# GpSimd's normalisation of attention rows: one instruction with two tensors, or four instructions with one scalar per row

## The chip, the cores and the metric

One core of one Trainium2 chip runs the whole program. The metric is the device time of one execution in microseconds; lower is better. The core has five engines, called here by the profile's names: PE (TensorE, matrix products), DVE (VectorE), ACT (ScalarE), POOL (GpSimd) and SP (SyncE, which here only issues DMA transfers). Each engine works through its own list of instructions in order and waits at the head of the list for what the next instruction needs.

## The reference

Sliding-window attention over 8 batches, 8 heads, 576 positions and head size 64, and behind it a two-layer network with squared ReLU over all 4608 tokens. All of it is float32.

```python
scores = scale * np.matmul(q, k.transpose(0, 1, 3, 2))
bias = slopes[:, None, None] * (-np.abs(rel).astype(np.float32))[None, :, :]
mask = (rel >= 0) & (rel < window)            # window = 128
scores = np.where(mask, scores + bias[None], -1000000000.0)
scores = scores - np.max(scores, axis=-1, keepdims=True)
attn = np.exp(scores)
attn = attn / (np.sum(attn, axis=-1, keepdims=True) + 1e-09)
out = np.matmul(attn, v)
x = out.transpose(0, 2, 1, 3).reshape(4608, 512)
h = np.maximum(x @ w_in, 0.0)                 # w_in 512 x 2048
return h * h @ w_out                          # w_out 2048 x 512
```

The division by the row sums is the step that the change touches. The kernel does it as a multiplication by reciprocals.

## The kernel before, in words

The 4608 tokens are cut into 9 chunks of 512. For each chunk the network needs 16 first products (`gemm1`, one per 128 of the 2048 hidden columns, 12 matmuls each, L200) and 16 second products (`gemm2`, L229, 12 matmuls each); `gemm2` of a hidden block runs two blocks behind its `gemm1`. Between the two, ACT takes the ReLU (`r`, L210), DVE squares it (`r<-r`, L213), ACT rounds it to a high part (`hh`, L217) and DVE takes the rest (`hl`, L219).

Attention is done in segments: a pair of heads times 256 tokens, held as a tile `t` of 128 query rows by 4 blocks of columns. Two segments, s = 0 and s = 1, make a `Couple`, and four couples make the input of one chunk. There are two forms.

- The first eight segments (`Wide`, in the first 40 us) are set out by a planner (`Plan.run`, `start`): it gives PE, DVE, ACT, POOL and SP an order by due times and its own costs. Here a row block has 256 columns (or 128 where the first half is masked away); the normalised blocks are turned by PE (L620, L623).
- From couple 4 on a segment's blocks have 128 columns each. DVE adds distances and takes maxima (L250), ACT takes exponentials with row sums (L257), DVE turns the four sums of a row into reciprocals (`nm`, L264 and L265), POOL multiplies the four blocks of `t` by them (`norm`, L268), DVE transposes 32 x 32 blocks of the result into `pp` (L319, STREAM_TRANSPOSE), SP writes that to DRAM in four transfers (`way<-pp`, L323) and reads it back in one (`pp<-way`, L328), and POOL cuts the square into its two triangles (two affine selects, L332).

From couple 9 on, past 150 us, the couples' matmuls come in a **visit** (function `visit`): once every 8 products, that is every 23.65 us, PE interrupts the network's products to multiply the old couple's triangles with the values (L539) and to make the new couple's scores (L546). The visit's new couple goes through the steps above during the 23 us that follow, s = 0 first, s = 1 behind it, and its four triangles are due at the next visit. There are 28 visits; called visit 0 (at 156.21 us) to visit 27 (at 797.63 us) here. Visits 1 to 27 each use a couple that passed through `norm` in the period before.

What stands around the change in each engine's list past 150 us: PE's order is written out by hand. The order of DVE, ACT, POOL and SP there is made by a scheduler that runs over the program with its own estimates of durations; a changed instruction can therefore move its neighbours. On SP the order within one period is: four writes of s = 0, the read of s = 0, four writes of s = 1, the read of s = 1. The writes of s = 1 stand behind the read of s = 0, which waits for its own writes to land.

The two functions of the change are `Segment.norm` (L267, the couples) and `Wide.norm` (L605, the first eight segments); segment 7 of these (`NORMS`) is normalised on DVE, one block at a time with a scalar per row, before and after.

Of the kernel before, what the change touches and what calls it, by code (L numbers as in the profile page):

```python
# [14 lines left out]
ALU = mybir.AluOpType  # L15
# [26 lines left out]
NORMS = (7,)  # L42
# [196 lines left out]
class Segment:  # L239
# [25 lines left out]
        self.nc.vector.reciprocal(rec, rec)  # L265

    def norm(self):  # L267
        self.nc.gpsimd.tensor_tensor(  # L268
            self.t, self.t, self.nm[:, 8:12].unsqueeze(2).to_broadcast([128, 4, 128]), op=ALU.mult
        )  # L270

    def turn(self):
        self.place()
# [285 lines left out]
class Wide(Segment):  # L559
# [45 lines left out]
    def norm(self):  # L605
        for i in (0, 1) if self.skip else (None,):
            m, a = (slice(None), 0) if i is None else (slice(i, 4, 2), self.first[i])
            t, rec = self.t[:, m, a:256], self.nm[:, 8:12][:, m]
            if self.k in NORMS:
                for j in range(t.shape[1]):  # L610
                    self.nc.vector.tensor_scalar(t[:, j], t[:, j], rec[:, j : j + 1], None, op0=ALU.mult)
                continue
            self.nc.gpsimd.tensor_tensor(t, t, rec.unsqueeze(2).to_broadcast(list(t.shape)), op=ALU.mult)

    def turn(self):
        self.place()
# [271 lines left out]
```

## Time and profile before

| | |
|---|---|
| median of 3 runs | 895.94 us (895.66 to 896.19) |
| profiled execution | 895.99 us |
| its span | 894.3 us |
| mean granted clock of PE | 0.999 |
| PE busy | 883.3 us (99%) |
| DVE / ACT / POOL busy | 496.7 / 419.0 / 200.0 us |
| `norm` of the couples (L268) | 64 instructions, 69.0 us busy |
| `norm` of the first segments (L613) | 11 instructions on POOL |

The profiled execution took 1.69 us more than the span of its instructions, and 0.05 us more than the median. A row of a timeline gives the start in us from the beginning of the span, the length in us, the engine, the line of the program, the operation with output and input, and how many instructions the row merges; in square brackets stands how long the engine was idle before it and what ended that. A row of the grouped view gives, after the bar, the busy time in us, the mean length of one instruction in ns, and the idle time before them. "SPq" marks SP's issuing of a transfer, not the transfer itself.

### The profile page before, as it was taken

The page shows a single profiled execution, that of the slowest core. Times are in us where ns is not written, and L with a number is a line of the kernel's source. Part 1 is how long each engine was busy: PE and PEld are TensorE (multiplying, and loading weights), DVE is VectorE, ACT ScalarE, POOL GpSimd, SP SyncE. Part 2 cuts the span into 40 slices and gives each one's busy share as a digit, 9 for nine tenths or more (in the row PEclk, how much of TensorE's full clock was granted, in tenths as well). Part 3 has the DMA queues.
Part 4 walks back from the last instruction along what each step waited for, and adds up shares of the span by engine and source line. Part 5 has one row for each costly group of instructions (what it writes and reads, how often), then busy time and mean ns, then how long its engine had stood idle before and what let it go on. Part 6 is the DMA issues. An engine that isn't in the chain of part 4 may idle for free.

```text
span 894.3 us, 19481 instructions
## 1 busy us (share of the span) xinstructions
PE 883.3 (99%) x7488; PEld 780.6 (87%) x7492; DVE 496.7 (56%) x1326; ACT 419.0 (47%) x1115; POOL 200.0 (22%) x255
## 2 busy tenths in 40 slices
PE   8899999999999999999999999999999999999998
PEld 5678888999899999999899989998999999989997
DVE  5999884555655555555545565555555555533222
ACT  7899753444444444334444444444444454323222
POOL 3222332222222222222222222212222222220000
PEclk9999999999999999999999999999999999999999
DMA  9985333332332334233422243333422331211001
GB/s 345 403 332 177 92 113 110 89 90 80 107 107 77 89 89 129 86 90 89 130 69 76 89 136 89 89 90 85 129 75 81 89 102 45 49 48 48 0 1 48
DMA packets 72893, 95.26 MB, mean 107 GB/s; under 512 B 8032, under 2 KB 41952, under 8 KB 72800
## 3 DMA queue, kind: packets, MB, share of 16 engines
q1 hardware_dynamic: 72368, 93.36, 33.9%
q8 instruction: 59, 0.97, 0.5%
q10 hardware_dynamic: 432, 0.66, 0.2%
q14 instruction: 34, 0.28, 0.1%
HBM read 67.76 MB, written 26.21 MB: 105 GB/s over the span
## 4 chain that ended last, share of the span: by engine, by line
PE 95%; ACT 3%; DVE 2%; issue 1%; POOLq 0%; DVEq 0%; ACTq 0%
PE acc L229 42%; PE g L200 42%; PE s L539 5%; PE g L546 2%; ACT tw L596 1%; PE s L546 1%; PE at L344 1%; PE g L132 0%; PE s L410 0%; ACT t L468 0%; PE at L410 0%; DVE tw L589 0%; DVE raw L178 0%; DVE pp L627 0%; ACT raw L176 0%
## 5 line engine op out<-in xcount | busy, mean ns | idle before, releaser
L200 PE MATMUL g<-xu,w 128*128 128x512 f32 x1728 | 400.9, 381 | 1.8 <-DVE xu L528 0.9
L200 PEld LDWEIGHTS g<-xu,w 128*128 128x128 f32 x1728 | 339.4, 197 | 39.6 <-DVE xu L528 2.3
L229 PE MATMUL acc<-hh,w 128*128 128x512 f32 x1152 | 371.1, 384 | 0.0
L229 PEld LDWEIGHTS acc<-hh,w 128*128 128x128 f32 x1152 | 225.9, 196 | 28.7 <-issue 5.3
L210 ACT ACTIVATE r<-g 128x512 f32<-128x512 f32 x144 | 86.0, 597 | 305.6 <-PE g L200 299.1
L229 PE MATMUL acc<-hl,w 128*128 128x512 f32 x576 | 219.2, 381 | 0.0
L213 DVE TENSOR_TENSOR r<-r 128x512 f32<-128x512 f32 x129 | 89.0, 690 | 225.7 <-ACT r L210 225.4
L219 DVE TENSOR_TENSOR hl<-r,hh 128x512 fp32r<-128x512 f32 x144 | 122.9, 854 | 78.3 <-ACT hh L217 78.1
L332 POOL TENSOR_SCALAR_AFFINE_SELECT pp<-pp 128x512 f32<-128x512 f32 x128 | 105.3, 823 | 230.2 <-DMA pp<-way 192.6
L217 ACT CAST hh<-r 128x512 fp32r<-128x512 f32 x144 | 89.2, 619 | 82.3 <-DVE r L213 80.8
L268 POOL TENSOR_TENSOR t<-t,nm 128x512 f32<-128x512 f32 x64 | 69.0, 1078 | 255.2 <-DVE nm L265 243.2
L229 PEld LDWEIGHTS acc<-hl,w 128*128 128x128 f32 x576 | 113.3, 197 | 11.6
L257 ACT ACTIVATE t<-t,nm 128x128 f32<-128x128 f32 x256 | 99.9, 393 | 12.2 <-DVE nm L250 12.1
L319 DVE STREAM_TRANSPOSE pp<-t 128x512 f32<-128x512 f32 x64 | 45.0, 705 | 35.9 <-POOL t L268 35.8
L250 DVE CUSTOM_DVE_ANT_0 t<-t,cst 128x128 f32<-128x128 f32 x256 | 59.1, 295 | 1.0
L539 PE MATMUL s<-pp,v 64*64 64x128 f32 (+1 forms) x1792 | 52.2, 248 | 0.1
L539 PEld LDWEIGHTS s<-pp,v 64*64 64x64 f32 x1792 | 40.7, 134 | 9.5 <-issue 8.4
L257 ACT ACTIVATION_READ_ACCUMULATOR t<-t,nm 128x1 f32 x256 | 48.3, 189 | 0.0
L480 DVE COPY_PREDICATED t<-cst,s 64x256 f32<-64x256 int32 x100 | 44.4, 444 | 6.5 <-ACT t L461 3.6
L527 ACT CAST xu<-s 128x512 fp32r<-128x512 f32 x28 | 16.4, 586 | 41.5 <-DVE t L480 26.6
L468 ACT COPY t<-g 64x256 f32<-64x256 f32 (+2 forms) x86 | 28.0, 340 | 3.9 <-PE g L546 1.2
L470 POOL MEMSET t<- 64x128 f32 (+1 forms) x44 | 10.0, 229 | 87.7 <-PE s L546 79.3
(71 smaller groups left out, 482.0 us busy)
## 6 DMA issues: line engine op xcount, KB each, us to landing
raw<-in_dram SPq DMA_DIRECT2D x32, 512.0 KB, 8.7
way<-pp SPq DMA_DIRECT2D x256, 64.0 KB, 2.0
pp<-way SPq DMA_DIRECT2D x64, 256.0 KB, 2.7
qk<-in_dram SPq DMA_DIRECT2D x32, 320.0 KB, 3.1
v<-in_dram SPq DMA_DIRECT2D x32, 320.0 KB, 3.9
qk<-in_dram SPq DMA_DIRECT2D x38, 256.0 KB, 4.2
out_dram<-o SPq DMA_DIRECT2D x35, 256.0 KB, 2.7
v<-in_dram SPq DMA_DIRECT2D x3, 256.0 KB, 4.9
```

Source lines behind the costliest of these rows:

```text
L200: nc.tensor.matmul(g, w, in_turn(c, xs[cc][:, part]), start=i == 0, stop=i == 11)
L210: self.relu = nc.scalar.activation(r, g, AF.Relu)
L213: nc.vector.tensor_tensor(r, r, r, op=ALU.mult)
L217: nc.scalar.copy(hh, r)
L219: nc.vector.tensor_tensor(hl, r, hh.bitcast(F32), op=ALU.subtract)
L229: nc.tensor.matmul(self.acc[m], w, in_turn(c, h), start=(f == 0 and i == 0), stop=(f == NF - 1 and i == 2))
L250: self.nc.vector.tensor_tensor_reduce(self.t[:, m], self.t[:, m], self.K.nrel(2 * self.p + m // 2), -0.125, BIG, ALU.add, ALU.min, self.nm ...
L257: return self.nc.scalar.activation(self.t[:, m], self.t[:, m], AF.Exp, bias=nm[:, m : m + 1], scale=-1.0, accum_out=nm[:, 4 + m : 5 + m],)
L268: self.nc.gpsimd.tensor_tensor(self.t, self.t, self.nm[:, 8:12].unsqueeze(2).to_broadcast([128, 4, 128]), op=ALU.mult)
L319: nc.vector.transpose(squares.rearrange("p b m c -> p m b c"), self.t.rearrange("p m (b c) -> p m b c", c=32))
L332: nc.gpsimd.affine_select(to, self.own, pattern=[[-32 * sign, 4], [0, 4], [-sign, 32]], compare_op=op, fill=0.0, base=0, channel_multiplie ...
L539: made.append(mm(to, w, x, start=first and n < 2, stop=not first, skip_group_check=True))
```

## The change

`norm` multiplies each of the four blocks by its own column of reciprocals, in four instructions whose second operand is one scalar per row, where one instruction (two in `Wide` segments with masked halves) took the tile and the reciprocals, repeated along the columns, as two tensors. What is multiplied by what is the same.

```diff
     def norm(self):
-        self.nc.gpsimd.tensor_tensor(
-            self.t, self.t, self.nm[:, 8:12].unsqueeze(2).to_broadcast([128, 4, 128]), op=ALU.mult
-        )
+        for m in range(4):
+            self.nc.gpsimd.tensor_scalar(self.t[:, m], self.t[:, m], self.nm[:, 8 + m : 9 + m], None, op0=ALU.mult)
...
             t, rec = self.t[:, m, a:256], self.nm[:, 8:12][:, m]
-            if self.k in NORMS:
-                for j in range(t.shape[1]):
-                    self.nc.vector.tensor_scalar(t[:, j], t[:, j], rec[:, j : j + 1], None, op0=ALU.mult)
-                continue
-            self.nc.gpsimd.tensor_tensor(t, t, rec.unsqueeze(2).to_broadcast(list(t.shape)), op=ALU.mult)
+            engine = self.nc.vector if self.k in NORMS else self.nc.gpsimd
+            for j in range(t.shape[1]):
+                engine.tensor_scalar(t[:, j], t[:, j], rec[:, j : j + 1], None, op0=ALU.mult)
```

Three lines fewer stand ahead of L613, so line numbers past it are lower by three in the changed program (L268 is L269, L319 is L318).

On POOL the couples' stretch stood as follows (t is a segment's probabilities, nm its sums and reciprocals, pp the transposed square):

```order
L332 AFFINE_SELECT pp<-pp 128x512 x4
L268 TENSOR_TENSOR t<-t,nm 128x512 x2
L470 MEMSET t 64x2x64 x2
L332 AFFINE_SELECT pp<-pp 128x512 x4
L268 TENSOR_TENSOR t<-t,nm 128x512 x2
```

and now stands:

```order
L331 AFFINE_SELECT pp<-pp 128x512 x4
L269 TENSOR_SCALAR t<-t,nm 128x128 x8
L469 MEMSET t 64x2x64 x2
L331 AFFINE_SELECT pp<-pp 128x512 x4
L269 TENSOR_SCALAR t<-t,nm 128x128 x8
```

Each pair of instructions became eight; nothing else on POOL moved. PE's and ACT's lists are the same as before. On DVE the lists are the same up to 140 us; past that, some neighbours of the STREAM_TRANSPOSE moved. Before, every couple's period had this order on DVE, from the last step of the old couple (xu) on:

```order
L528 TENSOR_TENSOR xu<-s,xu 128x512
L264 TENSOR_SCALAR nm<-nm 128x4
L265 RECIPROCAL nm<-nm 128x4
L319 STREAM_TRANSPOSE pp<-t 128x4x4x32
L213 TENSOR_TENSOR r<-r 128x512
L264 TENSOR_SCALAR nm<-nm 128x4
L265 RECIPROCAL nm<-nm 128x4
L219 TENSOR_TENSOR hl<-r,hh 128x512
L319 STREAM_TRANSPOSE pp<-t 128x4x4x32
L213 TENSOR_TENSOR r<-r 128x512
L219 TENSOR_TENSOR hl<-r,hh 128x512
```

In 13 of the 27 periods (those ahead of visits 12 to 21 and 24 to 26, **order A** in what follows) it still has. Ahead of visits 1 to 7 and 27 (**order B**) the square `r` stands ahead of the first transpose, and the rest is as before. Ahead of visits 8 to 11, 22 and 23 (**order C**) more moved:

```order
L527 TENSOR_TENSOR xu<-s,xu 128x512
L264 TENSOR_SCALAR nm<-nm 128x4
L265 RECIPROCAL nm<-nm 128x4
L213 TENSOR_TENSOR r<-r 128x512
L318 STREAM_TRANSPOSE pp<-t 128x4x4x32
L264 TENSOR_SCALAR nm<-nm 128x4
L219 TENSOR_TENSOR hl<-r,hh 128x512
L265 RECIPROCAL nm<-nm 128x4
L213 TENSOR_TENSOR r<-r 128x512
L318 STREAM_TRANSPOSE pp<-t 128x4x4x32
L219 TENSOR_TENSOR hl<-r,hh 128x512
```

There the second reciprocal, which lets POOL begin on s = 1, stands behind `hl`, and the second transpose stands behind the next block's `r`. Ahead of visit 8 a copy of an output tile (`o<-acc`, L235 before) stands ahead of that `r` too. On SP, about 150 us into the run, two output writes moved ahead of a read of `pp`; and in the period ahead of visit 8 two output writes, which stood behind the four writes of s = 1, now stand ahead of them, and two more ahead of the read of s = 1. The rest of its list is unchanged.

## The prediction

> **What bounds the kernel now.** I read the page first: the span, the busy times and the chain that ended last.
>
> ```profile
> span 894.3 us, 19481 instructions
> PE 883.3 (99%) x7488; PEld 780.6 (87%) x7492; DVE 496.7 (56%) x1326; ACT 419.0 (47%) x1115; POOL 200.0 (22%) x255
> PE 95%; ACT 3%; DVE 2%; issue 1%; POOLq 0%; DVEq 0%; ACTq 0%
> ```
>
> PE is idle for 11 us in all. POOL is on that chain with 0%. So a shorter `norm` can give back almost nothing, and a longer one costs only where its delay reaches PE. There are two such places: PE's transposes of the first segments, and the visits. Next the groups on POOL by form, which hold every duration from which the new instruction can be priced.
>
> ```profile
> L332 POOL TENSOR_SCALAR_AFFINE_SELECT pp<-pp 128x512 f32<-128x512 f32 x128 | 105.3, 823 | 230.2 <-DMA pp<-way 192.6 <-DVE r L213 11.4 <-DVE t L484 7.5
> L268 POOL TENSOR_TENSOR t<-t,nm 128x512 f32<-128x512 f32 x64 | 69.0, 1078 | 255.2 <-DVE nm L265 243.2 <-ACT r L210 7.0 <-ACT hh L217 4.0
> L470 POOL MEMSET t<- 64x128 f32 x32 | 6.4, 199 | 53.6 <-PE s L546 45.2 <-PE at L410 4.4 <-DVE pp L319 3.3
> L613 POOL TENSOR_TENSOR tw<-tw,nm 128x1024 f32<-128x1024 f32 x3 | 5.7, 1895 | 2.4 <-PE acc L297 1.7 <-DVE nm L603 0.7
> L470 POOL MEMSET t<- 64x256 f32 x12 | 3.7, 308 | 34.1 <-PE s L546 34.1
> L182 POOL CAST w<-raw 128x1024 fp32r<-128x1024 f32 x3 | 3.4, 1135 | 9.3 <-DVE raw L180 3.4 <-ACT t L461 3.2 <-ACT tw L596 2.7
> L613 POOL TENSOR_TENSOR tw<-tw,nm 128x256 f32<-128x256 f32 x4 | 2.5, 613 | 11.2 <-DVE nm L603 11.2
> ```
>
> Then the timeline of one period, the one ahead of visit 8 (346.59 us), without the rows that carry nothing here.
>
> ```profile
> 331.02 1.04 POOL L268 TENSOR_TENSOR t<-t,nm 128x512 f32<-128x512 f32 x1 [6.14 <-DVE nm L265]
> 331.16 0.60 ACT L210 ACTIVATE r<-g 128x512 f32<-128x512 f32 x1 [0.70 <-PE g L200]
> 332.10 0.71 DVE L319 STREAM_TRANSPOSE pp<-t 128x512 f32<-128x512 f32 x1 [1.23 <-POOL t L268]
> 332.74 0.65 DVE L213 TENSOR_TENSOR r<-r 128x512 f32<-128x512 f32 x1
> 332.84 1.77 SPq L323 DMA_DIRECT2D way<-pp  x4
> 333.52 0.18 DVE L265 RECIPROCAL nm<-nm 128x4 f32<-128x4 f32 x1
> 333.85 1.04 POOL L268 TENSOR_TENSOR t<-t,nm 128x512 f32<-128x512 f32 x1 [1.78 <-DVE nm L265]
> 334.07 1.36 DVE L219 TENSOR_TENSOR hl<-r,hh 128x512 fp32r<-128x512 f32 x1 [0.37 <-ACT hh L217]
> 335.36 0.70 DVE L319 STREAM_TRANSPOSE pp<-t 128x512 f32<-128x512 f32 x1
> 336.07 0.34 SPq L328 DMA_DIRECT2D pp<-way  x1
> 336.34 0.60 ACT L210 ACTIVATE r<-g 128x512 f32<-128x512 f32 x1 [2.30 <-PE g L200]
> 336.50 1.84 SPq L323 DMA_DIRECT2D way<-pp  x4
> 336.99 0.69 DVE L235 COPY o<-acc 128x512 f32<-128x512 f32 x1 [0.93 <-PE acc L229]
> 338.39 0.91 SPq L236 DMA_DIRECT2D out_dram<-o  x2
> 338.96 0.69 DVE L219 TENSOR_TENSOR hl<-r,hh 128x512 fp32r<-128x512 f32 x1
> 340.09 0.33 SPq L328 DMA_DIRECT2D pp<-way  x1
> 344.14 1.04 POOL L332 TENSOR_SCALAR_AFFINE_SELECT pp<-pp 128x512 f32<-128x512 f32 x1
> 346.59 0.62 PE L539 MATMUL s<-pp,v 64*64 64x64 f32 x20
> ```
>
> Three things are to be seen. The first transpose (332.10) starts 0.04 us behind POOL's end, so `norm` of s = 0 is on the way to the triangles, and SP writes at once behind it. The writes of s = 1 (336.50) stand on SP behind the read of s = 0 (336.07), which waits for the writes of s = 0; the second transpose ended at 336.06, so it has 0.4 us to spare there. And `hl` took 1.36 us beside POOL's `norm` and 0.69 us alone: it waited until POOL's instruction was over (334.89) and then ran.
>
> How much a visit can take is read from the last pair of affine selects and the start of PE's L539 behind it. These are the tight visits, 3, 10 and 20:
>
> ```profile
> 225.51 1.52 POOL L332 TENSOR_SCALAR_AFFINE_SELECT pp<-pp 128x512 f32<-128x512 f32 x2 [4.32 <-DMA pp<-way]
> 227.15 0.66 PE L539 MATMUL s<-pp,v 64*64 64x64 f32 x21
> 392.19 1.53 POOL L332 TENSOR_SCALAR_AFFINE_SELECT pp<-pp 128x512 f32<-128x512 f32 x2 [3.92 <-DMA pp<-way]
> 393.89 0.33 PE L539 MATMUL s<-pp,v 64*64 64x64 f32 x5
> 629.73 1.52 POOL L332 TENSOR_SCALAR_AFFINE_SELECT pp<-pp 128x512 f32<-128x512 f32 x2 [3.14 <-DMA pp<-way]
> 631.11 0.76 PE L539 MATMUL s<-pp,v 64*64 64x64 f32 x17
> ```
>
> Visit 20 began 0.14 us before its last triangle ended (631.25), and it was late: that triangle held it. An undisturbed pair takes 1.52 us, so PE waits as soon as the pair begins later than 1.38 us ahead of the visit. The **room** of a visit is what is left to that: 0.26 us at visit 3, 0.32 at visit 10, 0 at visit 20; 1.87 at visit 8, whose pair began at 343.34 and was held up in its second half by a `hl`. The other 23, worked out in the same way, have 1.0 (visit 17) to 2.6 us (visit 11).
>
> **The price of the new instruction.** No row shows it. The two-tensor form takes 613 ns for 256 columns and 1895 for 1024: 1.67 ns a column and 0.185 us fixed. Memsets take 199 and 308 ns for 128 and 256: 0.85 ns a column and 0.09 fixed, but they read nothing. The cast reads and writes one tensor: 1135 ns for 1024, at 0.85 a column 0.26 fixed. The select goes likewise: an undisturbed pair of 1.52 is 0.76 each, 0.325 fixed. For 128 columns that is 0.20 us at least (memset) and 0.54 at most (two-tensor slope, the select's fixed part). I take the cast's: 0.11 + 0.26 = 0.37, because it too reads one tensor. Four make 1.48 against 1.04: **+0.44 us for each `norm`** (from -0.24 to +1.12). That POOL is then busy 28 us longer in all costs nothing by itself: POOL is busy 22% of the span.
>
> **The first segments.** With 256 columns an instruction costs 0.22 + 0.26 = 0.48, four 1.92 against 1.895; with masked halves 2 x 0.37 + 2 x 0.48 = 1.70 against 1.61. PE's transposes have more than that:
>
> ```profile
> 9.21 1.61 POOL L613 TENSOR_TENSOR tw<-tw,nm 128x256 f32<-128x256 f32 x2 [8.30 <-DVE nm L603]
> 12.96 0.66 PE L620 MATMUL at<-cst,tw 128*128 128x128 f32 x4
> 15.36 3.46 POOL L613 TENSOR_TENSOR tw<-tw,nm 128x256 f32<-128x256 f32 x3 [1.97 <-DVE nm L603]
> 17.95 0.66 PE L620 MATMUL at<-cst,tw 128*128 128x128 f32 x4
> 20.22 0.60 PE L620 MATMUL at<-cst,tw 128*128 128x128 f32 x4
> ```
>
> For the first segment 2.1 us lie between POOL's end (10.82) and the transposes; for segments 2 and 3, one behind the other on POOL (to 15.36 + 1.61 = 16.97, and to 18.82), 1.0 and 1.4. The cover is the score products and ACT's exponentials ahead of them. I put 0 here; without the cover it would be 0.1 us per segment.
>
> **The steady periods, by order.** *Order A* (13 periods). The first transpose, hence SP's chain, moves by +0.44. For s = 1, `hl` begins beside POOL as before, but now it gets in behind the first of four instructions: POOL needs 0.37, waits about 0.62 for `hl`, and needs 1.11 more, 2.1 in all, where the second transpose began 1.51 behind POOL's start. With the first 0.44 that is +1.03, less the 0.4 to spare: the writes of s = 1 move by **+0.65**.
>
> On the lock the row stands above (1.36 against 0.69). The Trainium skill, "SBUF — State Buffer", "Who interferes with whom", says that a VectorE instruction with two SBUF inputs and a GpSimd instruction that reads SBUF take a shared port for a whole instruction each, the first to start blocking the other; that is what the row shows. It does not say who gets the port between two GpSimd instructions in a row; if POOL keeps it through all four, the second transpose begins 0.15 us earlier than I put it.
>
> *Order B* (8 periods). `r` now runs ahead of the first transpose, and so beside `norm` of s = 0: its ReLU is ready at 331.76, in the midst of POOL's four, and its 0.65 us comes on top of them. The first transpose moves by 0.44 + 0.65, **+1.1**, and SP's chain with it; s = 1 follows within that.
>
> *Order C* (6 periods). The second transpose stands behind the next block's `r`, and that waits for a ReLU which ends at 336.94 (PE sets it, so POOL doesn't move it). `r` runs 336.97 to 337.6, and the transpose begins 2.24 us later than at 335.36; less 0.4 that is **+1.8**. Ahead of visit 8 a copy of 0.69 stands between too, and on SP two output writes (0.91) that wait for ACT's copy: the writes of s = 1 go out at 339.25, **+2.75**.
>
> Behind those writes nothing changes: landing, read, pair of selects. What the move takes beyond the room is PE's wait: visit 3 (B) 1.1 - 0.26 = 0.84; visit 8 (C) 2.75 - 1.87 = 0.88; visit 10 (C) 1.8 - 0.32 = 1.48; visit 20 (A) 0.65; the other 23 nothing (nearest is visit 6, order B, with 1.04 of room: 0.06). The DVE rows that move are not waited for by PE: `hl` is used two blocks later. **Sum: 0.84 + 0.88 + 1.48 + 0.65 + 0.06 = 3.9 us.** On the profiled execution's 895.99 that is 899.9; against the median of 895.94 it is +0.44%.
>
> With 0.20 us per instruction visit 20 and most of visit 3 fall away (0.15 left), while visits 8 and 10, set by the order, stay: +2.5, 898.5. With 0.54 order A moves by about 2.0 and B by 2.0, C by 2.6 to 3.1: some 17 visits lose 14 us together, 910.
>
> **The rivals.** (1) *The room is found where it is not now.* Visits 3, 10 and 20 are tight because their last read landed late (visit 10's pair begins 1.70 us ahead of its visit, visit 8's 3.25, out of the same steps). If a late landing belongs to its moment, a moved chain misses it. Then visit 8 alone pays: about +0.9, 896.9, no change that can be told. For it speaks that only 3 of 27 are tight; against it, that these three recur in a program whose runs agree within 0.03%, and that the orders B and C put all their visits nearer. (2) *Not slower: four short instructions beat one long one.* POOL reads one tensor where it read two, and pays 0.85 for 1.67 ns a column; if the fixed part of each is hidden behind the one before, four take 4 x 0.11 + 0.26 = 0.70, 0.34 less than now. This is decided at a length of 0.26 us per instruction: below, `norm` is shorter. The Trainium skill, "GPSIMD Engine Reference", 3.1 and 4.1, speaks for it: one-input work near one column a cycle, two-input work at about 2.5 cycles; the memsets agree with the first (0.85 ns), the two-tensor rows are cheaper than the second (1.67 ns, where 2.5 cycles at the page's 1.2 GHz are an estimate of 2.1). It would bring visit 20 forward by up to that, against the two visits that the order sets; with these landing better, 895.99 - 0.34, 895.6. (3) *The instruction is dear*, 0.54 us or more, because each has to fetch its scalar before it starts: 910 and above, as worked out. Nothing in the trace shows such a fetch on POOL.
>
> **How the numbers follow.** The forecast 0.47 (898 to 904), rival 1 0.32, rival 2 0.07, rival 3 0.14. A measurement here tells 0.2% (1.8 us) from no change. Slower: the forecast, rival 3 and a little of rival 1, 0.63; no change: the rest of rival 1 and nearly half of rival 2, 0.33; faster 0.04. The range, 896.2 to 906, holds the forecast, most of rival 1 and leaves rival 3 out.
>
> **What would show it.** POOL's group of L269: 256 instructions near 370 ns, and starts near that apart where DVE is quiet. The first transpose 0.4 us later in A and 1.1 in B against its visit; the second behind a ReLU in C. PE's waits at L538 (before L539) appearing at visits 3, 8, 10 and 20 and nowhere else; PE's list and the first 50 us as they are. Wrong would be: instructions far from 0.37 us, waits spread over all visits, or a first matmul of the network that starts later.

## The result, and the profile after

The change takes **905.43 us** (median of 4 runs, 903.94 to 907.14), where the kernel before took 896.07 beside it (4 runs, 895.66 to 896.79). That is 1.0104 times as long, interval 1.008 to 1.0128: slower by 9.4 us. The forecast was slower by 3.9 us, 899.9, in a range that reached to 906. So the direction held, and the median lies in the range, but two of the four executions (906.74 and 907.14) lie above it; the size did not hold: it fell short by more than half.

The profiled run of the change took 903.94 us, and its span is 7.9 us longer than that of before. It is the fastest of the four, so 1.5 of the median's 9.4 us are not in it. First the page of the change: span, busy times, and the chain that ended last.

```profile
span 902.2 us, 19709 instructions
PE 887.6 (98%) x7492; PEld 782.2 (87%) x7492; DVE 474.0 (53%) x1326; ACT 417.6 (46%) x1115; POOL 307.5 (34%) x464
PE 78%; DVE 5%; DMA 4%; POOL 4%; ACT 2%; SPq 1%; issue 1%; POOLq 0%; DVEq 0%; ACTq 0%
```

POOL, which had 0% of the chain, now has 4%, and it is busy 307.5 us where it was busy 200.0. The forecast was 28 us more, not 107. Where these come from is in the groups on POOL by form:

```profile
L269 POOL TENSOR_SCALAR t<-t,nm 128x128 f32<-128x128 f32 x256 | 170.2, 680 | 245.2 <-DVE nm L265 243.2 <-ACT hh L217 2.1
L610 POOL TENSOR_SCALAR tw<-tw,nm 128x256 f32<-128x256 f32 x20 | 19.1, 971 | 0.0
L610 POOL TENSOR_SCALAR tw<-tw,nm 128x128 f32<-128x128 f32 x8 | 4.7, 601 | 8.1 <-DVE nm L602 8.1
```

An instruction of 128 columns takes 0.60 us where it is undisturbed (the mean of 680 at L269 holds those that ran beside VectorE), and one of 256 columns 0.97. Four of the first kind take 2.34 us from first to last against the 1.04 of the instruction that they replace: **+1.30 us for each `norm`**, three times the forecast. In the first segments the work was 12.4 us before: 2.5 and 5.7 for the forms of 256 and 1024 columns, and 4.2 for this one, of the groups of before:

```profile
L613 POOL TENSOR_TENSOR tw<-tw,nm 128x512 f32<-128x512 f32 x4 | 4.2, 1041 | 0.0
```

Now it is 23.8 (19.1 + 4.7).

PE loses its time in two places. The waits of PE (in all, how often, the longest, in us) name them:

```profile
PE at L617 <- POOL tw L610: 3.0, 4, 1.0
PE s L538 <- POOL pp L331: 2.1, 6, 0.7
```

**The first segments.** The windows of the second and third ten microseconds (columns after the length: PE, PEld, DVE, ACT and POOL busy), first of before, then of the change:

```profile
10.00:20.00 10.00, 9.70 (x85) 6.51 (x87) 7.00 (x39) 9.87 (x39) 6.90 (x7) 1.00 1.05 397
20.00:30.00 10.00, 9.49 (x90) 6.73 (x92) 8.73 (x32) 9.71 (x33) 5.06 (x5) 1.00 1.03 404
```

```profile
10.00:20.00 10.00, 9.86 (x86) 6.29 (x84) 6.94 (x37) 9.82 (x39) 10.00 (x13) 1.00 1.04 398
20.00:30.00 10.00, 8.01 (x70) 5.18 (x68) 6.54 (x25) 8.22 (x28) 10.00 (x13) 1.00 1.03 404
```

POOL was busy 6.9 and 5.1 us of ten, and is now full. Its timeline has it as one row, 28 instructions without a break; under it one of PE's rows where it stood still ahead of a transpose, and the first product of the network:

```profile
9.01 23.63 POOL L610 TENSOR_SCALAR tw<-tw,nm 128x128 f32<-128x128 f32 x28 [8.12 <-DVE nm L602]
```

```profile
29.23 0.33 PE L617 MATMUL at<-cst,tw 128*128 128x128 f32 x1 [1.04 <-POOL tw L610]
40.12 3.03 PE L200 MATMUL g<-xu,w 128*128 128x512 f32 x12
```

That product begins at 40.12 us where it began at 37.14 before. That is **+2.98 us**, as much as PE's four waits at L617.

**The visits.** From there on PE's list has a fixed pace, and what it loses is seen in the distance between the first matmuls (L538) of two visits, against the same distance before. A loss stands at the visit whose triangles were late. In us:

```
visit    3     5     6     7     8    12    13    17    20    24   others | sum
loss   0.56  0.60  0.55  0.24  0.84  0.07  0.41  0.32  0.29  0.98    0    | 4.87
```

The row of PE's waits at L538 has only 2.1 of the 4.87, because a matmul that is under way is booked as busy for a part of the stop: at visit 24 two of its matmuls start 0.89 us apart, and 0.67 of that is booked as idle. 2.98 + 0.1 (up to visit 0) + 4.87 are the 7.95 by which PE ends later. The forecast had 0 for the first part and 3.9 for the second, at visits 3, 8, 10, 20 and 6.

The period ahead of visit 8, which the prediction followed row by row, stands so in the timeline of the change:

```profile
336.13 2.54 POOL L269 TENSOR_SCALAR t<-t,nm 128x128 f32<-128x128 f32 x4 [6.31 <-DVE nm L265]
336.81 0.80 DVE L213 TENSOR_TENSOR r<-r 128x512 f32<-128x512 f32 x1 [0.86 <-ACT r L210]
338.70 0.71 DVE L318 STREAM_TRANSPOSE pp<-t 128x512 f32<-128x512 f32 x1 [1.09 <-POOL t L269]
339.44 1.77 SPq L322 DMA_DIRECT2D way<-pp  x4
340.31 2.34 POOL L269 TENSOR_SCALAR t<-t,nm 128x128 f32<-128x128 f32 x4 [1.64 <-DVE nm L265]
342.62 0.68 DVE L213 TENSOR_TENSOR r<-r 128x512 f32<-128x512 f32 x1
343.22 0.70 DVE L318 STREAM_TRANSPOSE pp<-t 128x512 f32<-128x512 f32 x1
344.06 2.38 SPq L322 DMA_DIRECT2D way<-pp  x4
350.88 1.52 POOL L331 TENSOR_SCALAR_AFFINE_SELECT pp<-pp 128x512 f32<-128x512 f32 x2 [3.68 <-DMA pp<-way]
351.62 0.33 PE L538 MATMUL s<-pp,v 64*64 64x64 f32 x2
352.46 0.79 PE L538 MATMUL s<-pp,v 64*64 64x64 f32 x27 [0.52 <-POOL pp L331]
```

Against the visit (now 351.62, before 346.59) the first transpose is 1.57 us later, the second 2.83, the writes of s = 1 2.53 and the last pair of selects 2.51. The pair begins 0.74 us ahead of the visit, and PE waits in its midst.

How late the pair is says all of what a visit loses. With its **lead**, the time by which the pair begins ahead of the visit, the loss is 1.57 us less the lead, and nothing where the lead is longer: 0.98 at visit 24 (lead 0.59), 0.32 at visit 17 (1.26), nothing at visit 10 (1.62). This holds at every visit from 1 to 26 of this profile within 0.1 us (at visit 20, 0.19 was lost before too), and so it does in the profiles of the change again, of the couples alone, of the old order, of the four instructions of the old form and of e2_twice, all told below.

### The profile page after: what moved, and what is told of

Read it like the earlier page. It is cut to its first block, busy times and chain, and to the rows that moved or that the text cites. A ratio compares the mean times of both kernels' runs of the same rounds, so it can differ in the third digit from the quotient of the medians.

```text
span 902.2 us, 19709 instructions
## 1 busy us (share of the span) xinstructions
PE 887.6 (98%) x7492; PEld 782.2 (87%) x7492; DVE 474.0 (53%) x1326; ACT 417.6 (46%) x1115; POOL 307.5 (34%) x464
## 4 chain that ended last, share of the span: by engine, by line
PE 78%; DVE 5%; DMA 4%; POOL 4%; ACT 2%; SPq 1%; issue 1%; POOLq 0%; DVEq 0%; ACTq 0%
PE acc L229 35%; PE g L200 34%; PE s L538 5%; POOL t L269 3%; PE g L545 2%; DMA pp<-way 2%; DMA way<-pp 2%; POOL pp L331 1%; SPq L322 1%; PE s L545 1%; ACT t L467 1%; DVE t L479 1%; DVE pp L318 1%; ACT t L257 1%; PE at L343 1%
## 5 line engine op out<-in xcount | busy, mean ns | idle before, releaser
L269 POOL TENSOR_SCALAR t<-t,nm 128x128 f32<-128x128 f32 x256 | 170.2, 680 | 245.2 <-DVE nm L265 243.2
L213 DVE TENSOR_TENSOR r<-r 128x512 f32<-128x512 f32 x129 | 91.7, 711 | 197.4 <-ACT r L210 197.3
L331 POOL TENSOR_SCALAR_AFFINE_SELECT pp<-pp 128x512 f32<-128x512 f32 x128 | 99.8, 780 | 182.6 <-DMA pp<-way 136.9
L219 DVE TENSOR_TENSOR hl<-r,hh 128x512 fp32r<-128x512 f32 x144 | 100.4, 697 | 68.0 <-ACT hh L217 66.8
L318 DVE STREAM_TRANSPOSE pp<-t 128x512 f32<-128x512 f32 x64 | 45.4, 710 | 102.7 <-POOL t L269 86.9
L538 PE MATMUL s<-pp,v 64*64 64x128 f32 (+1 forms) x1792 | 55.2, 248 | 2.4 <-POOL pp L331 2.1
L538 PEld LDWEIGHTS s<-pp,v 64*64 64x64 f32 x1792 | 42.5, 133 | 12.7 <-POOL pp L331 8.0
```

What stands on the lines that cost most here:

```text
L213: nc.vector.tensor_tensor(r, r, r, op=ALU.mult)
L219: nc.vector.tensor_tensor(hl, r, hh.bitcast(F32), op=ALU.subtract)
L269: self.nc.gpsimd.tensor_scalar(self.t[:, m], self.t[:, m], self.nm[:, 8 + m : 9 + m], None, op0=ALU.mult)
L318: nc.vector.transpose(squares.rearrange("p b m c -> p m b c"), self.t.rearrange("p m (b c) -> p m b c", c=32))
L331: nc.gpsimd.affine_select(to, self.own, pattern=[[-32 * sign, 4], [0, 4], [-sign, 32]], compare_op=op, fill=0.0, base=0, channel_multiplie ...
L538: made.append(mm(to, w, x, start=first and n < 2, stop=not first, skip_group_check=True))
```

## The experiments

Two theories stood after the result. **Length:** everything comes from the 0.60 us of the new instruction, at the two places. **Order:** the visits lose because VectorE's rows moved (orders B and C), and the instruction's length only brings the first part. The first set was timed in five rounds on one chip; before took 896.12 us there.

**The change again**, as the measure for the others.

> The whole change once more, as the measure for the next three on the same chip. Both theories: 1.008 to 1.013 of the kernel before (904 to 907 us). The theory of length says that the scalar instruction's own duration (0.60 us for 128 columns, 0.97 for 256, from the profile after) makes all of it; the theory of order says that the moved transposes and reciprocals on VectorE (orders B and C) make most of what the visits lose.

905.79 us, 1.0108 (1.0093 to 1.0122). Its profiled run has the first product 3.5 us later, 0.7 more up to visit 0, and 5.8 at the visits: 3, 5, 6, 7, 8, 13, 21 and 24 in the main. The visits that lose are mostly the same; the amounts move by some tenths, at visit 21 by 0.85.

**The first segments alone.** `Wide.norm` as in the change, the couples as before.

```
 Segment.norm: nc.gpsimd.tensor_tensor(t, t, reciprocals, op=mult)            (as before)
 Wide.norm:    for j: engine.tensor_scalar(t[:, j], t[:, j], rec[:, j], mult) (as changed)
```

> Only the first eight segments take the scalar form; the couples keep one instruction with two tensors. Length: +3.0 us (the matmuls of the network began 2.98 us later in the profile after, and nothing behind 40 us differs here), ratio 1.0033. As the prediction had it (first segments covered): +0, ratio 1.000. Order says nothing on this part.

899.78 us, **1.0042** (1.0031 to 1.0054), +3.7 us. The first product is 3.62 us later, and the visits lose nothing (-0.05 in all). Among the waits of PE stands now:

```profile
PE at L618 <- POOL tw L611: 3.4, 5, 1.0
```

The prediction put 0 here.

**The couples alone**, the reverse. VectorE keeps order A in 24 of 27 periods.

> Only the couples take the scalar form. VectorE's list then keeps order A in 24 of 27 periods (B once, C twice). Length: the visits lose nearly what they lost with the whole change, +4 to +6 us, ratio 1.0045 to 1.0065; the sum with the run on the first segments gives the whole change. Order: with the old order in 24 periods most of the loss is gone, +0 to +2 us, ratio 1.000 to 1.002.

900.72 us, **1.0055** (1.0043 to 1.0067). The visits lose 3.9 us, the first product nothing (-0.19). So with nearly no row moved the visits lose four fifths of what they lose in the change's first profile. The two halves together make 0.97%, the whole 1.08% on the same chip: nearly the sum. Where the small rest comes from is not settled.

**The change, with VectorE in the old order.** Each square `r` is tied behind the last transpose, so that orders B and C are gone; in 7 periods something still stands otherwise: in five a step of 128 x 4, ahead of visits 4 and 8 a copy of an output tile (`o<-acc`, 0.69 us) in front of the second transpose.

```
+ self.K.turned = nc.vector.transpose(squares, ...)
  sq = nc.vector.tensor_tensor(r, r, r, op=ALU.mult)
+ if self.turned is not None and self.big:
+     self.tc.add_manual_dep(sq.ins, self.turned.ins.name, ORDER)
```

> The whole change, but each square on VectorE is tied behind the transpose that stood ahead of it before, so that orders B and C are gone (in 8 periods a small step or a copy still stands one place off). Length: no difference from the whole change, ratio 1.008 to 1.013. Order: the loss of the visits ahead of which B or C stood goes (visits 3, 5, 6, 7 and 8, 2.8 us in the profile after), ratio 1.005 to 1.009.

907.23 us, 1.0124 (1.0111 to 1.0137): not better than the change. The waits of PE grew at the visits:

```profile
PE s L543 <- POOL pp L336: 3.8, 8, 0.8
```

The theory of the order falls: with the moved rows put back, the visits of the profiled run lose 8.0 us, not less than the change's 4.9 and 5.8. Without visits 4 and 8, where the copy stands in the way, it is 6.5 against 4.0 and 4.6.

**The prices by themselves.** Behind the last visit, where nothing else is to be done, the kernel before was given pairs of instructions on a spare tile: unused work, the outputs are as before. (The loops are left out here.)

```
+ P.tensor_scalar(y, y, one[:, m:m+1], None, op0=mult)    # L845: a scalar per row; 128, 256, 512 columns
+ P.tensor_scalar(y, y, 1.0, None, op0=mult)              # L849: a constant; 128, 512
+ P.tensor_tensor(y, y, one column repeated, op=mult)     # L853: 128, 512
+ P.tensor_tensor(y, y, y, op=mult)                       # L857: 128, 512
+ P.tensor_copy(y, z)                                     # L859: 128, 512, once each
```

> The kernel before, and behind its last affine select POOL multiplies and copies columns of a spare tile: the scalar form with a scalar per row (128, 256 and 512 columns) and with one constant (128, 512), the two-tensor form with the repeated column and with two full tensors (128, 512), a copy (128, 512). PE doesn't wait for any of it: 896 us. If the dear part is the loop over columns, the scalar form costs 0.60, 0.97 and 1.7 us (2.9 ns a column) and the constant the same; if it is the fetch of the scalar, the constant is shorter by a fixed part and both have the same slope; if the form is as the prediction took it, 512 columns cost 0.7. The two-tensor form at 128 columns: 0.40 either way.

One run, 896.83 us. The groups on POOL by form:

```profile
L845 POOL TENSOR_SCALAR pp<-pp,nm 128x512 f32<-128x512 f32 x2 | 3.1, 1572 | 0.0
L849 POOL TENSOR_SCALAR pp<-pp 128x512 f32<-128x512 f32 x2 | 3.0, 1497 | 0.0
L853 POOL TENSOR_TENSOR pp<-pp,nm 128x512 f32<-128x512 f32 x2 | 2.1, 1045 | 0.1
L845 POOL TENSOR_SCALAR pp<-pp,nm 128x256 f32<-128x256 f32 x2 | 1.9, 932 | 0.0
L845 POOL TENSOR_SCALAR pp<-pp,nm 128x128 f32<-128x128 f32 x2 | 1.2, 608 | 0.1
L849 POOL TENSOR_SCALAR pp<-pp 128x128 f32<-128x128 f32 x2 | 1.0, 537 | 0.0
L857 POOL TENSOR_TENSOR pp<-pp 128x128 f32<-128x128 f32 x2 | 0.8, 400 | 0.1
L859 POOL COPY pp<-pp 128x512 f32<-128x512 f32 x1 | 0.6, 613 | 0.1
```

The scalar form takes (1572 - 608) / 384 = **2.5 ns a column** and 0.29 us besides. With a constant in place of the row's scalar it is (1497 - 537) / 384 = 2.5 ns again and 0.22 fixed. So a scalar per row costs 0.07 us more than a constant, and the slope is the instruction's own. With two tensors it is (1045 - 400) / 384 = 1.7 ns, and 0.185 fixed. (The two rows of two tensors that are not shown, L853 at 128 and L857 at 512 columns, each hold one instruction that ran beside VectorE: 862 ns where the other took 399, and 1502 where the other took 1047.) The form that multiplies one tensor takes half as long again per column as the form that multiplies two. It is not the count of tensors that sets it: the copy reads and writes one tensor too, and takes 0.61 us for 512 columns, near the 0.7 that the prediction's price gives, where a multiplication by a constant takes 1.50.

**Four instructions of the old form** in the couples: the split without the scalar form; the first segments as before.

```
- nc.gpsimd.tensor_tensor(t, t, nm[:, 8:12] repeated to 128x4x128, op=mult)
+ for m in range(4):
+     nc.gpsimd.tensor_tensor(t[:, m], t[:, m], nm[:, 8+m] repeated to 128x128, op=mult)
```

> The couples in four instructions as in the change, but each in the two-tensor form (one column of reciprocals repeated over 128 columns); the first segments as before. If the scalar form is what is dear: 0.40 us each, 1.6 us for four where the scalar form takes 2.34, and +0.5 to +2.5 us, ratio 1.0005 to 1.003. If it is the splitting into four (handing over, the port shared four times), then as the couples alone with scalars: +4.6 us, ratio 1.0055.

897.31 us, 1.0011 (1.0002 to 1.0021); before took 896.19 in this set. The rows of its line give the length:

```profile
L269 POOL TENSOR_TENSOR t<-t,nm x256: 392/399/1428, 52.1 to 788.8; 128x128 f32<-128x128 f32 x128
```

The median is 399 ns, two thirds of 601. Four take 1.47 us from first to last where nothing runs beside them. The visits of the profiled run lose 1.06 us, 0.86 of it at visit 24. So the split alone costs 0.1%, and the rest of the couples' 0.55% goes with the scalar form's length.

**POOL's `norm` lengthened by other means.** If length is all, then the old instruction with a second one behind it that multiplies by ones must cost the same. It was made with half the tile (e2_one_and_half) and with the whole of it (e2_twice); the outputs stay what they are.

```
  nc.gpsimd.tensor_tensor(t, t, reciprocals, op=mult)
+ nc.gpsimd.tensor_tensor(t[:, 0:n], t[:, 0:n], ones repeated, op=mult)    # n = 2 or 4
```

> The couples in one two-tensor instruction as before, and behind it half of the tile once more times a tile of ones: no scalar form, no four pieces, only 0.61 us more on the way to the transpose. Length: the visits lose what their room does not hold, +1 to +2.5 us, ratio 1.001 to 1.003. A theory in which the scalar form disturbs VectorE or the order rather than being long: +0, ratio 1.000.

918.73 us, 1.0256 (1.0236 to 1.0276): a miss, far outside either theory. The timeline of POOL in one of the bad periods shows why:

```profile
168.55 1.04 POOL L270 TENSOR_TENSOR t<-t,nm 128x512 f32<-128x512 f32 x1 [1.75 <-DVE nm L267]
173.48 0.73 POOL L337 TENSOR_SCALAR_AFFINE_SELECT pp<-pp 128x512 f32<-128x512 f32 x1 [3.89 <-DMA pp<-way]
174.17 0.61 POOL L273 TENSOR_TENSOR t<-t,ones 128x256 f32<-128x256 f32 x1
```

The order written for POOL put a select between the two multiplications of s = 1. It waited 3.9 us for the read of s = 0, and the second multiplication, the transpose and the writes stood behind it. Five periods were so, those ahead of visits 1, 2, 3, 21 and 27. The first four of these visits lost 14.2 us, and 4.2 more went at visit 27 and behind it. PE stood still for 1.9 to 2.3 us at the first three, for 3.2 at visit 21 and for 2.5 at visit 27. Around the end of the last two stops the granted clock stood at 0.50 for 3.4 us (670.5 to 673.9 and 817.3 to 820.7); around the other three it stayed at 1.00. The other visits lost 2.5, and 0.5 went ahead of visit 0: a little more than length let expect (1 to 2.5), but the run as a whole proves nothing on it.

> As the run before, with the whole tile once more times ones: about 2.1 to 2.2 us on the way to the transpose, close to the 2.34 of four scalar instructions. Length: +3.5 to +5 us, ratio 1.004 to 1.0055, about what the couples alone lost with scalars (1.0055). The other theory: +0, ratio 1.000.

903.09 us, 1.0077 (1.0062 to 1.0092), +6.9; 1.004 to 1.0055 had been expected. Its visits lose 4.1 us, of which 1.10 at visit 17 and 0.93 at visit 24, near the couples' 3.9. Another 2.76 us go between the first product and visit 0, where the change lost 0.1 to 0.7; 0.9 of them is one wait of PE for a step on POOL's list (L413, at 93.4 us). Length accounts for the first part; the rest of the second stays open.

**The same four instructions on VectorE**, so that POOL has no `norm` in the couples at all. Length expects the loss to vanish, and asks whether a shorter way wins anything.

```
+ for m in range(4):
+     nc.vector.tensor_scalar(t[:, m], t[:, m], nm[:, 8+m], None, op0=mult)
```

> The couples' four multiplications with a scalar per row on VectorE in place of GpSimd, as one of the first segments has it before and after (340 ns for 256 columns there); the first segments as before. Length, its other side: the way from reciprocals to transpose gets shorter (four of about 0.2 us, no handing over to GpSimd and back), the visits have nothing to lose and next to nothing to win, -0.5 to +0.3 us, ratio 0.9994 to 1.0003. If it is the scalar form or the splitting into four as such that costs the visits, it shows here too: +2 to +5 us, ratio 1.002 to 1.0055.

896.49 us against 896.30, **1.0002** (0.9993 to 1.0011): as before. The group on VectorE:

```profile
L269 DVE TENSOR_SCALAR t<-t,nm 128x128 f32<-128x128 f32 x256 | 56.0, 284 | 2.0
```

284 ns against 601 on POOL for the same operation and tile, and PE never waits for POOL. The first transpose stands about 0.3 us earlier against its visit than before (median of the 27). But the kernel is no faster than before, which bears out the prediction's first reading: a shorter `norm` has nothing to give back. No version here beats the kernel before.

## Why the prediction was right, and where it was wrong

**The price: the step that failed first.** "I take the cast's: 0.11 + 0.26 = 0.37, because it too reads one tensor." Measured: 0.60, and above even the upper bound of 0.54. The bound was built from the steepest slope in the trace (1.67 ns a column) and the largest fixed part (0.325). The fixed part held (0.29); the slope is 2.5. No row of before holds a scalar form on POOL that does arithmetic, and the count of tensors read said nothing on it. The Trainium skill, "GPSIMD Engine Reference", 4.1, calls one-input work on GpSimd "roughly line-rate". The prediction's second rival drew on that; the rows at L845 and L849 speak against it for a multiplication, and the measurement decides (the copy's 0.61 us for 512 columns does not speak against it).

**The first segments: 0 put, 3 to 3.7 us found.** This was one third of the loss. The step compared four instructions of 0.48 with one of 1.895 and found 0.1 us "without the cover". With 0.97 and 0.60 it is 3.9 against 1.9 for a full segment and 3.1 against 1.6 for one with masked halves, and the cover of 1.0 to 2.1 us is used up in the fourth, where PE waits first (at 21.30 us). The price alone is not the whole fault: the share of 22% over the span hid that POOL was already busy 69% and 51% in these windows. At twice the work it is full, and each segment is later than the one before. The prediction had named "a first matmul of the network that starts later" as a sign that it was wrong.

**The chain of order A: right, with two wrong prices in it.** Put the measured 2.34 for four instructions in place of 1.48 into the prediction's own formula. The first transpose moves by 1.3, the second by 1.30 + 2.34 + 0.62 - 1.51 = 2.75, the writes of s = 1 by 0.4 less, 2.35. Measured, against the visit: ahead of visit 12, +1.32 and +2.43 for the transposes; the writes went from 10.0 us ahead to 8.0 ahead. What is too much by 0.3 to 0.4 is the 0.62 that POOL was to wait for `hl`.

**The lock: right in kind, too dear.** That `hl` gets in behind a short instruction was a step of the forecast. Where it does, one of the four takes 0.81 to 0.90 us in place of 0.60, and `hl` itself waits less. So POOL waits 0.2 to 0.3 us for it, not 0.62. Its group before and after:

```profile
L219 DVE TENSOR_TENSOR hl<-r,hh 128x512 fp32r<-128x512 f32 x144 | 122.9, 854 | 78.3 <-ACT hh L217 78.1
```

```profile
L219 DVE TENSOR_TENSOR hl<-r,hh 128x512 fp32r<-128x512 f32 x144 | 100.4, 697 | 68.0 <-ACT hh L217 66.8 <-PE s L545 0.7
```

The mean falls from 854 to 697 ns, almost what it takes alone (0.69). The Trainium skill, "SBUF — State Buffer", "Who interferes with whom", describes the lock for one instruction against one. That the port is free to VectorE between two GpSimd instructions in a row is what these rows add. In e2_twice, with two long ones in a row, it is seen best: `hl` begins at 435.25, beside the first of them (435.00 to 436.04), and ends at 436.59, and the second takes 1.37 us in place of 1.04.

**Orders B and C: the terms of their own were wrong.** Their 1.1, 1.8 and 2.75 us were a sum of price and order. Visit 8 lost 0.84, where 0.88 was forecast, and its writes moved by 2.53 against 2.75: the size fits, the reason does not. The second transpose waited for `norm`: that began 1.43 us later against the visit and took 1.30 longer, 2.73 of the 2.83 by which the transpose is later. The square ahead of it ended 0.65 us behind the end of `norm`, where `hl` before had ended 0.54 behind it: it cost the rest, 0.1, and not the 2.24 of a late ReLU, which had ended 0.7 us ahead of the end of `norm`. A moved row is hidden if what it was moved past has become later by as much. The old order restored gained nothing.

**The room: wrong as a list, and too dear as a sum.** With writes 2.0 us late, the rooms of the thirteen order-A visits would give 4.6 us (2.0 at visit 20, 1.0 at 17, 0.9 at 13, 0.7 at four others). Measured: 2.07, with 0.29 at visit 20 and 0.98 at visit 24. With the moves that the writes of all 27 periods in fact made, the rooms would give 9.0 in place of 4.87. Two things were wrong in the step. The limit of 1.38 us was taken from visit 20, which had itself lost 0.19 (it is 23.94 us to the next visit there, and 23.75 in e3_on_dve, where its triangles were in time); by the losses above it is 1.57, so every other room was 0.19 smaller. And "Behind those writes nothing changes" did not hold: the landings changed. This is seen at visits 10 and 24. SP's rows and the pair, first before, then in the change (visit 10 begins at 393.89 and 399.76, visit 24 at 726.33 and 733.29; the first two rows of the change at visit 24 are of s = 0):

```profile
384.13 1.81 SPq L323 DMA_DIRECT2D way<-pp  x4
389.29 0.34 SPq L328 DMA_DIRECT2D pp<-way  x1
392.19 1.53 POOL L332 TENSOR_SCALAR_AFFINE_SELECT pp<-pp 128x512 f32<-128x512 f32 x2 [3.92 <-DMA pp<-way]
...
716.27 2.30 SPq L323 DMA_DIRECT2D way<-pp  x4
720.00 0.33 SPq L328 DMA_DIRECT2D pp<-way  x1
723.11 1.84 POOL L332 TENSOR_SCALAR_AFFINE_SELECT pp<-pp 128x512 f32<-128x512 f32 x2 [2.66 <-DMA pp<-way]
```

```profile
392.06 1.82 SPq L322 DMA_DIRECT2D way<-pp  x4
395.28 0.34 SPq L327 DMA_DIRECT2D pp<-way  x1
398.14 1.52 POOL L331 TENSOR_SCALAR_AFFINE_SELECT pp<-pp 128x512 f32<-128x512 f32 x2 [2.25 <-DMA pp<-way]
...
720.86 3.24 SPq L322 DMA_DIRECT2D way<-pp  x4
725.55 0.34 SPq L327 DMA_DIRECT2D pp<-way  x1
725.99 1.81 SPq L322 DMA_DIRECT2D way<-pp  x4
729.57 0.33 SPq L327 DMA_DIRECT2D pp<-way  x1
732.70 1.52 POOL L331 TENSOR_SCALAR_AFFINE_SELECT pp<-pp 128x512 f32<-128x512 f32 x2 [2.48 <-DMA pp<-way]
```

Ahead of visit 24 the writes are 2.76 us later against the visit, not 2.0, because the read of s = 0 ahead of them came 4.70 us behind its own writes, where it came 3.23 behind them before (712.61 to 715.84). The pair is 2.63 later: nearly all is passed on. Of the room of 1.84 nothing is left, and 0.98 is lost. At visit 20 it is the other way round: the read of s = 0 came 4.68 us behind its writes before and 3.96 in the change, and the writes of s = 1 moved by only 0.59. Ahead of visit 10 the writes are 2.06 us later and the pair only 0.08: the read followed the writes after 5.16 us before and after 3.22 now, so the late landing did not come again. That is the first rival's mechanism. It holds for some visits and not for others: where a landing got better, a visit was spared in all or in part (10, 20), and others that had seemed roomy paid: 24 for a landing that got worse, and 5, 6 and 13 because their writes moved further than forecast.

The four instructions of the old form show the same step at the forecast's own length: their `norm` takes 1.47 us undisturbed (forecast 1.48), and the writes of s = 1 move by 0.44 (median; forecast 0.65). There visits 3, 10 and 20 lose nothing, and 0.86 us goes at visit 24, whose writes came 2.40 later.

**The rivals.** The first was half right, as just said; its 896.9 fell. The second fell with the price: a split in the cheaper form cost 0.1% and the scalar form 0.55% in the couples alone. The third had the right price and the wrong reason: a scalar per row costs 0.07 us more than a constant, the slope is what is dear. Its 910 was too high: it had 14 us at the visits, with every landing as it was, where 4.87 were lost.

So the likeliest case failed first in one number, the price, and through it in the cover of the first segments. That the median lies in the range is in part luck: the price was too low and the first segments stood at 0, while the wait for `hl` and the sum over the visits were taken too dear, and these errors pull in opposite directions.

## What to carry to other kernels

Price an instruction only from a row of its own form on its own engine; where there is none, a bound made of other forms' slopes is no bound, and a scalar form on GpSimd may cost half as much again per column as the two-tensor form it replaces. Read an engine's share in the stage that the change touches and multiply it there: 22% over the span was 69% in the window where it mattered. Room that one execution shows ahead of a DMA's landing does not name the visits that will pay, and here, taken as a sum, it gave about twice the loss (9.0 us against 4.87).

## What the runs showed of the hardware that was not expected

- On GpSimd a multiplication of one tensor by a scalar (2.5 ns a column, row's scalar or constant alike) is slower than one of two tensors (1.7 ns); a scalar per row costs only 0.07 us more than a constant, and a copy of 512 columns takes 0.61 us in all, against 1.50 for a multiplication by a constant.
- A waiting VectorE instruction is let in between GpSimd instructions in a row, so that four short ones cost VectorE less than one long one (`hl` 697 ns against 854), though they hold POOL two and a quarter times as long.
- In e2_one_and_half PE stood still five times for more than 1.9 us. Around the end of the two longest stops (2.5 and 3.2 us) the granted clock was 0.50 for 3.4 us; around the other three (1.9 to 2.3 us) it stayed at 1.00.
- The first 40 us shift by themselves: in three of the second set's kernels (e2_prices, e2_four_two_tensor, e2_twice), which differ from before only later on but for one small memset, the first product came 0.85 us later than in the trace of before, and in the fourth 0.17 earlier. So of the 2.98 to 3.62 us above, each single profile is good to about 0.9; the medians of the runs (+3.7 for the first segments alone) are the better measure.
- From the writes of a square to the read that follows them it took 5.16 us at one visit and 3.22 at the same visit in another program, with as many writes; what sets it was not settled by these runs.
